# Talking-heads attention and two MoE layers on one core: the first two chunks relaid out by two queues, six score products moved behind the first mixing, one load of values moved to the front

## The chip, the core and the metric

The kernel runs on one core of a Trainium2 chip. Its engines are TensorE (PE: matmuls, with weight loads shown apart as PEld), VectorE (DVE), ScalarE (ACT), GpSimd (POOL) and SyncE (SP). SP, ACT and POOL can each start DMAs; in the profile an issue is listed under SPq, ACTq or POOL, and it is not counted as busy time of the engine. The metric is the device time of one execution in microseconds, the median of the timed runs.

## The reference

Everything is float32. For each of 2 batches, 12 heads, 448 positions and 64 numbers per head:

```python
scores = scale * q @ k.T                                 # per head
scores = einsum('bhij,hg->bgij', scores, w_pre)          # mix the 12 heads
attn   = softmax(scores)                                 # over j
attn   = einsum('bhij,hg->bgij', attn, w_post)           # mix them again
x      = attn @ v                                        # 896 tokens x 768
x = (silu(x @ w_gate) * (x @ w_val)) @ w_out             # 768 -> 1536 -> 768
h = x @ w_in ; x = (h * relu6(h + 3) / 6) @ w_out2       # 768 -> 2048 -> 768
```

The attention is less than the first third of the time; all that the change touches lies in its first steps.

## The kernel before

The program is written out engine by engine in the order in which the Python code issues it; no scheduler reorders it, and semaphores are put in where one engine reads what another writes. So the order of the code is the order on each engine.

**Attention, tile by tile.** Each batch is cut into four tiles of about 120 query rows, eight tiles in all (t = 0 to 7). `scores(t, c)` makes the products of q and k for head pair c (six pairs, c = 0 to 5) in two PSUM banks; `scores_out(t, c)` copies them to the SBUF tile `S` of that t, one head by DVE and one by ACT. There are two `S` tiles, used in turn, so tile 2 writes where tile 0 was. As heads have to be mixed, the heads of ten query rows (a chunk) must come to lie over the partitions of one matmul: `relayout(m)` copies eight rows' heads of chunk m from `S` to `sx` by one DMA (104 partitions, 182 KB, issued by SP), and `relayout_rest(m)` the last two rows' (24 partitions, 42 KB, issued by POOL). Below, the first is called the main relayout and the second the rest. Tile 0 has the chunks 0 to 9, tile 1 begins with chunk 10. Two chunks make a pair.

`next_engines(n)` is a tiny DMA by POOL that moves the place at which POOL's next DMA begins among the 16 DMA engines.

**The steps.** The loop at L615 runs over steps i from -2. In step i PE does `postmix(i)` (second mixing of pair i) and `premix(i + 2)` (first mixing of pair i + 2), DVE does `weights(i + 1)` and `row_max(i + 2)`, ACT does `exps(i + 1)`. For one pair the path is: both mains and both rests landed, `premix` on PE (four matmuls), `row_max` on DVE (two TENSOR_REDUCE, L252), `exps` on ACT (L261), `weights` on DVE (three small operations), `postmix` on PE (L287), `attn_out` (copies, L306), later `av` (L318). Other work hangs on named places in a step: `at_step(i, f, ..., place=...)`. The scores of tile 2 are made in steps 1 to 5, and its first copy to `S` must wait until all relayouts of tile 0 have landed.

**What is fixed before the loop.** The loads of q, k, the mixing weights and two of four pieces of v (`load_v(0, 0)` and `(0, 1)`, L139) are issued; then all scores of tiles 0 and 1 (L527 to L530); between them the relayouts of chunks 0 to 7 are issued. From step -2 on further relayouts follow, two or three per step; `scored[t]` (L555) is the step after which those of tile t may be issued, and the first one of a step waits for that step's `postmix`, the others for its `row_max`. The third and fourth piece of v are issued by ACT in steps 1 and 2, `load_q(3)` by ACT in step 3 (L594).

**Counters.** DMAs of SP and ACT use eight completion counters in turn (DMAHW0 to DMAHW7 in the listings). A DMA that gets a counter first waits until the DMA that had it before, eight earlier in the program, has landed. What stands behind such a DMA on its engine waits with it.

After the attention come the matmuls of the MoE layers (L441), to which nothing is done here.

Of the kernel before, what the change touches and what calls it, by code (L numbers as in the profile page):

```python
# [16 lines left out]
B, H, S, D = 2, 12, 448, 64  # L17
NT = B * S
DM = H * D
HP = H // 2  # L20
# [7 lines left out]
JC = 4  # L28
# [20 lines left out]
def kernel(  # L49
# [14 lines left out]
    nc = tc.nc  # L64
# [5 lines left out]
    def bank(name, tag):  # L70
        return ps.tile([128, 512], F32, name=name, tag=tag, bufs=BUFS[tag])
# [18 lines left out]
    small = kp.tile([128, 8], F32, name="small")  # L90
# [23 lines left out]
    def new_v(b):  # L114
        vs[b] = pv.tile([128, JC, H, D], F32, name=f"v{b}", tag="v")

    def load_v(b, j, eng=nc.scalar):
        eng.dma_start(
            out=vs[b][:, j].rearrange("p h d -> p (h d)"), in_=vv[b, :, j * DM : (j + 1) * DM]
        )  # L120
# [15 lines left out]
    nc.sync.dma_start(out=W2.rearrange("p g k -> p (g k)"), in_=w_post)  # L136
    load_q(2, eng=nc.sync)
    new_v(0)
    for j in range(2):  # L139
        load_v(0, j, nc.sync)  # L140

    Ss = [psc.tile([128, H + 1, S], F32, name=f"S{i}") for i in range(2)]
# [14 lines left out]
    stiles, pqk = {}, {}  # L157

    def scores(t, c, tags=("pqk", "pqk")):

        b, i = divmod(t, 4)
        n = ROWS[b][i]
        if c == 0:
            stiles[t] = Ss[t % 2]
        base = c * n
        p = [bank(f"pqk{t}_{c}_{e}", tags[e]) for e in range(2)]
        for s in range(2):
            lo, hi = 64 * s, min(64 * s + 64, n)
            for e in range(2):
                r = slice(64 * e, 64 * e + 64)  # L170
                nc.tensor.matmul(  # L171
                    p[e][lo:hi, :S],
                    lhsT=qs[t][r, base + lo : base + hi],
                    rhs=ks[b][r, c, :],
                    start=True,
                    stop=True,
                    tile_position=(64 * e, 64 * s),
                )
        for e in range(2):
            pqk[t, 2 * c + e] = p[e]  # L180

    def scores_out(t, c):
        n = ROWS[t // 4][t % 4]
        for e in range(2):
            h = 2 * c + e
            copy = nc.scalar.copy if e else nc.vector.tensor_copy
            copy(stiles[t][:n, h, :], pqk.pop((t, h))[:n, :S])  # L187

    sx = {}

    in_turn = mybir.DependencyInfo(mybir.DependencyClass.Sync, mybir.DependencyReason.DATA)

    def relayout(m, then=None):

        t, c = chunks[m]
        i, r = divmod(m, 2)  # L200
        if r == 0:
            sx[i] = psx.tile([128, 2, S], F32, name=f"sx{i}", tag="sx")
        rows = stiles[t][c : c + 7 * STRIDE + 1 : STRIDE, :, :]
        dma = nc.sync.dma_start(out=sx[i][0:104, r, :], in_=rows)
        if then:
            tc.add_manual_dep(dma.ins, then, in_turn, reason="a step's share of the DMA engines")

    def next_engines(n):

        to = 4 + n % 4  # L210
        nc.gpsimd.dma_start(
            out=small[0:24, to : to + 1], in_=small[0:8, 0:3].rearrange("p (h w) -> p h w", w=1)
        )

    next_engines(0)

    def relayout_rest(m):
        t, c = chunks[m]
        rows = stiles[t][c + 8 * STRIDE : c + 9 * STRIDE + 1 : STRIDE, :H, :]
        nc.gpsimd.dma_start(out=sx[m // 2][104:128, m % 2, :], in_=rows)  # L220
        if m % 4 == 3 and m + 1 < NCH:
            next_engines(m // 4 + 1)

# [105 lines left out]
    turns = cst.tile([1, 1], F32, name="turns")  # L329
# [189 lines left out]
    def keep_clock(n):  # L519

        p = ps.tile([128, 512], F32, name=f"clock{n}", tag="ppost", bufs=BUFS["ppost"])
        for _ in range(n):
            nc.tensor.matmul(p[:, :480], lhsT=ones[0], rhs=ones[1], start=True, stop=True)

    keep_clock(WARM)
    placed = 0
    for t in range(2):  # L527
        for c in range(HP):
            scores(t, c, (("pqk", "pqk"), ("ppre", "ppre"), ("ppost", "ppost"), ("ppre", "pav"))[(6 * t + c) % 4])
            scores_out(t, c)  # L530
        if t == 0:
            for _ in range(8):
                relayout(placed)
                relayout_rest(placed)
                placed += 1
    rests = placed

# [3 lines left out]
    def at_step(i, f, *args, place="end"):  # L541
        extra[i][place].append((f, args))
# [9 lines left out]
        else:  # L552
            at_step(now + 1, scores_out, t, c, place="S")

    scored = {0: -3, 1: -3}  # L555
    for t in range(2, 8):
        scored[t] = 6 * t - 7
        for c in range(HP):
            i = scored[t] - 5 + c
# [8 lines left out]
    for t, (begin, end) in enumerate(((5, 10), (11, 16), (17, 22), (23, 28), (29, 34), (35, 40), (41, 46))):  # L568
        busy = None
        for c in range(HP):  # L570
            i = begin + c * (end - begin + 1) // HP
            out = x_out if t < 6 else x_last
# [11 lines left out]
        if t < 6:  # L584
            step = 1 if t < 4 else 2
            i = split_at.setdefault(t, max(end + 1, split_at.get(t - 1, 0) + 4 // step))
# [4 lines left out]
    at_step(20, new_v, 1)  # L591
    for b in range(2):
        at_step(scored[4 * b + 3] + 1, new_x, b)
    loads = [(1, load_v, 0, 2), (2, load_v, 0, 3), (3, load_q, 3), (6, load_q, 4)]  # L594
    loads += [(7 + n, load_k, 1, n, n + 1) for n in range(HP)]
    loads += [(15, load_q, 5), (21, load_q, 6), (27, load_q, 7)]
    loads += [(20 + 2 * j, load_v, 1, j) for j in range(JC)]
# [17 lines left out]
    for i in range(-LOOK, NP):  # L615
# [36 lines left out]
        for m in ready[:1]:  # L652
            relayout(m, begun_at)
        run(i, "end")
        for m in ready[1:]:
            relayout(m, maxed)
        placed += len(ready)

        while rests < placed and rests // 2 <= i + LOOK + 4 and i > scored[chunks[rests][0]]:
            relayout_rest(rests)  # L660
            rests += 1
# [181 lines left out]
```

## Time and profile before

| | |
|---|---|
| time, median of 3 runs | 673.52 us (673.15 to 676.69) |
| the profiled execution | 671.94 us |
| its span, first to last instruction | 670.2 us |
| PE busy in the span | 659.1 us (98%) |
| granted TensorE clock, mean | 1.000 of full |

The span is what the rows below count in: microseconds from the first instruction. The 1.7 us between span and time of the execution lie around it. The profile names an instruction by its line, its engine and its operands; "idle before" and "<-" say how long the engine stood before it and which event ended that. The chain of work that ended last goes back from the last instruction, at each step to what released it.

### The profile page before, as it was taken

The page shows a single profiled execution, that of the slowest core. Times are in us where ns is not written, and L with a number is a line of the kernel's source. Part 1 is how long each engine was busy: PE and PEld are TensorE (multiplying, and loading weights), DVE is VectorE, ACT ScalarE, POOL GpSimd, SP SyncE. Part 2 cuts the span into 40 slices and gives each one's busy share as a digit, 9 for nine tenths or more (in the row PEclk, how much of TensorE's full clock was granted, in tenths as well). Part 3 has the DMA queues.
Part 4 walks back from the last instruction along what each step waited for, and adds up shares of the span by engine and source line. Part 5 has one row for each costly group of instructions (what it writes and reads, how often), then busy time and mean ns, then how long its engine had stood idle before and what let it go on. Part 6 is the DMA issues. An engine that isn't in the chain of part 4 may idle for free.

```text
span 670.2 us, 16126 instructions
## 1 busy us (share of the span) xinstructions
PE 659.1 (98%) x6680; PEld 561.8 (84%) x6680; DVE 499.8 (75%) x836; ACT 296.5 (44%) x603; POOL 160.4 (24%) x204
## 2 busy tenths in 40 slices
PE   8999999999999999999999999999999999999997
PEld 2456665666899999999999999999999998999996
DVE  4878888889278888887886666578888888775540
ACT  4567776777244343433432323244445543333220
POOL 3544466545111122111120000013333332000000
PEclk9999999999999999999999999999999999999999
DMA  7767576545024242332432434222223333554420
GB/s 253 218 200 210 178 219 192 181 142 198 3 94 141 95 141 95 112 124 95 135 100 95 132 104 134 102 94 97 94 95 101 119 96 100 178 155 122 145 67 27
DMA packets 35225, 86.87 MB, mean 130 GB/s; under 512 B 10096, under 2 KB 23040, under 8 KB 35152
## 3 DMA queue, kind: packets, MB, share of 16 engines
q1 hardware_dynamic: 21600, 71.43, 32.3%
q10 hardware_dynamic: 5616, 10.48, 5.1%
q0 software_dynamic: 7936, 3.94, 2.4%
q8 instruction: 52, 0.85, 0.6%
q14 instruction: 21, 0.17, 0.1%
HBM read 62.37 MB, written 2.75 MB: 97 GB/s over the span
## 4 chain that ended last, share of the span: by engine, by line
PE 94%; DMA 3%; DVE 2%; ACT 1%; issue 0%; ACTq 0%; SPq 0%; DVEq 0%
PE pi L441 17%; PE pp L441 17%; PE po L441 13%; PE pv L441 12%; PE pg L441 12%; PE pav L318 5%; PE ppost L287 5%; PE ppre L239 4%; PE pqk L171 4%; PE p L441 2%; PE pav L337 2%; DMA sx<-S 2%; DMA k<-in_k_dram 1%; ACT e L261 1%; DVE nm L252 0%
## 5 line engine op out<-in xcount | busy, mean ns | idle before, releaser
L441 PE MATMUL pp<-g,hp 128*128 128x448 f32 x384 | 107.9, 362 | 0.0
L703 POOL TENSOR_TENSOR g<-rl,g 128x448 fp32r<-128x448 f32 x32 | 41.4, 1313 | 167.9 <-ACT g L702 167.9
L441 PE MATMUL po<-u,ho 128*128 128x448 f32 x288 | 81.3, 363 | 0.0
L441 PEld LDWEIGHTS pp<-g,hp 128*128 128x128 f32 x384 | 71.9, 187 | 4.5 <-ACT hp L427 0.2
L261 ACT ACTIVATE e<-ppre,nm 128x448 f32<-128x448 f32 x90 | 56.3, 631 | 35.4 <-DVE nm L252 33.8
L441 PE MATMUL pp<-g,lp 128*128 128x448 f32 x192 | 69.7, 363 | 0.2 <-DVE lp L432 0.2
L441 PE MATMUL pi<-x2l,hi 128*128 128x448 f32 x192 | 69.7, 363 | 0.0
L441 PE MATMUL pi<-x2h,hi 128*128 128x448 f32 x192 | 69.6, 362 | 0.0
L441 PE MATMUL pi<-x2h,li 128*128 128x448 f32 x192 | 69.1, 360 | 0.0
L703 POOL TENSOR_TENSOR u<-sg,u 128x448 fp32r<-128x448 f32 x24 | 32.2, 1362 | 148.3 <-ACT u L702 148.3
L220 POOL DMA_DIRECT2D sx<-S x90 | 52.5, 584 | 49.5 <-issue 11.8
L441 PEld LDWEIGHTS po<-u,ho 128*128 128x128 f32 x288 | 54.1, 188 | 3.5
L252 DVE TENSOR_REDUCE nm<-ppre 128x1 f32<-128x448 f32 x90 | 51.9, 618 | 4.8 <-PE ppre L239 2.3
L287 PE MATMUL ppost<-wn,e 60*64 60x60 f32 x2520 | 51.0, 220 | 3.0 <-DVE wn L273 1.7
L441 PE MATMUL po<-u,lo 128*128 128x448 f32 x144 | 51.8, 360 | 0.0
L318 PEld LDWEIGHTS pav<-at,v 128*64 128x64 f32 x576 | 27.9, 136 | 28.4 <-ACT xs L360 14.2
L239 PE MATMUL ppre<-sx,W 64*64 64x448 f32 x360 | 49.7, 544 | 1.3 <-ACT S L187 0.6
L287 PEld LDWEIGHTS ppost<-wn,e 60*64 60x64 f32 x2520 | 45.1, 134 | 6.1 <-ACT at L306 2.0
L171 PE MATMUL pqk<-k,q 64*64 64x448 f32 (+3 forms) x384 | 47.8, 539 | 1.2 <-DMA k<-in_k_dram 0.6
L441 PE MATMUL pg<-xl,hg 128*128 128x448 f32 x132 | 47.9, 363 | 0.0
L441 PE MATMUL pv<-xl,hv 128*128 128x448 f32 x132 | 47.9, 363 | 0.0
L441 PE MATMUL pg<-xh,hg 128*128 128x448 f32 x132 | 47.8, 362 | 0.0
(98 smaller groups left out, 1399.1 us busy)
## 6 DMA issues: line engine op xcount, KB each, us to landing
sx<-S SPq DMA_DIRECT2D x90, 182.0 KB
ri<-in_moe_w_in_dram SPq DMA_DIRECT2D x16, 768.0 KB
ro<-in_moe_w_out_dram SPq DMA_DIRECT2D x12, 768.0 KB
rg<-in_moe_w_gate_dram SPq DMA_DIRECT2D x11, 768.0 KB
rv<-in_moe_w_val_dram SPq DMA_DIRECT2D x11, 768.0 KB
rp<-in_moe_w_out_dram SPq DMA_DIRECT2D x12, 640.0 KB
rp<-in_moe_w_out_dram SPq DMA_DIRECT2D x6, 768.0 KB
sx<-S POOLq DMA_DIRECT2D x90, 42.0 KB, 4.5
```

The costliest lines, as they stand in the source:

```text
L171: nc.tensor.matmul(p[e][lo:hi, :S], lhsT=qs[t][r, base + lo : base + hi], rhs=ks[b][r, c, :], start=True, stop=True, tile_position=(64 * e ...
L220: nc.gpsimd.dma_start(out=sx[m // 2][104:128, m % 2, :], in_=rows)
L239: nc.tensor.matmul(p[a][64 * r : 64 * r + 64, :S], lhsT=W1[rows, :], rhs=x[rows, r, :], start=True, stop=True, tile_position=(64 * a, 64 * r),
L252: top = nc.vector.tensor_reduce(nm[:, a : a + 1], pre[i][a][:, :S], AX.X, ALU.max, negate=True)
L261: nc.scalar.activation(e2[a], p[a][:, :S], AF.Exp, bias=nm[:, a : a + 1], scale=1.0, accum_out=sm[:, a : a + 1])
L287: mm = nc.tensor.matmul(p[s][64 * c : 64 * c + 64, at, :, :], lhsT=e2[a][rows, 64 * k : 64 * k + 64], rhs=wn[rows, a, :].rearrange("p (g k ...
L318: nc.tensor.matmul(p[64 * e : 64 * e + 64, : 2 * n], lhsT=vs[b][:, jc, h, :], rhs=ats[t][:, 2 * jc : 2 * jc + 2, h, :n], start=jc == 0, st ...
L337: mm = nc.tensor.matmul(pavs[t, c][64 * e : 64 * e + 64, a * n : a * n + n], lhsT=vs[b][rows, JC - 1, h, :], rhs=ats[t][rows, KB - 1, h, : ...
L441: nc.tensor.matmul(p[:, :S], lhsT=wt[:, kk, :], rhs=xx, start=start, stop=stop)
L703: eng.tensor_tensor(to[1], src, to[0].bitcast(F32), ALU.subtract)
```

## The change

Four edits, all in the first steps.

1. `load_v(0, 2)`, the third piece of v (384 KB), is issued by SP with the first two, ahead of the relayouts, and no longer by ACT in step 1.
2. The main relayout of chunk 1 is issued by ACT, behind its copies of tile 0; SP issues the main of chunk 0 and then, in POOL's place, the rest of chunk 0. The first `next_engines` moves 16 elements, no longer 24.
3. `scores(1, 5)`, the last of tile 1, is made by PE in step -2 behind `premix(0)`, and its copies by DVE and ACT in step -1. The PSUM banks of the scores are given by a table, since the banks come round in another order.
4. `scored[1]` goes from -3 to -1, so that the relayouts of tile 1 (chunk 10 on) are issued from step 0 on, no longer from step -1.

```diff
--- before.py
+++ after.py
@@ -136,7 +136,7 @@
     nc.sync.dma_start(out=W2.rearrange("p g k -> p (g k)"), in_=w_post)
     load_q(2, eng=nc.sync)
     new_v(0)
-    for j in range(2):
+    for j in range(JC - 1):
         load_v(0, j, nc.sync)
 
     Ss = [psc.tile([128, H + 1, S], F32, name=f"S{i}") for i in range(2)]
@@ -190,7 +190,7 @@
 
     in_turn = mybir.DependencyInfo(mybir.DependencyClass.Sync, mybir.DependencyReason.DATA)
 
-    def relayout(m, then=None):
+    def relayout(m, then=None, eng=nc.sync):
 
 
 
@@ -201,23 +201,23 @@
         if r == 0:
             sx[i] = psx.tile([128, 2, S], F32, name=f"sx{i}", tag="sx")
         rows = stiles[t][c : c + 7 * STRIDE + 1 : STRIDE, :, :]
-        dma = nc.sync.dma_start(out=sx[i][0:104, r, :], in_=rows)
+        dma = eng.dma_start(out=sx[i][0:104, r, :], in_=rows)
         if then:
             tc.add_manual_dep(dma.ins, then, in_turn, reason="a step's share of the DMA engines")
 
-    def next_engines(n):
+    def next_engines(n, turns=3):
 
         to = 4 + n % 4
         nc.gpsimd.dma_start(
-            out=small[0:24, to : to + 1], in_=small[0:8, 0:3].rearrange("p (h w) -> p h w", w=1)
+            out=small[0 : 8 * turns, to : to + 1], in_=small[0:8, 0:turns].rearrange("p (h w) -> p h w", w=1)
         )
 
-    next_engines(0)
-
-    def relayout_rest(m):
+    next_engines(0, 2)
+
+    def relayout_rest(m, eng=nc.gpsimd):
         t, c = chunks[m]
         rows = stiles[t][c + 8 * STRIDE : c + 9 * STRIDE + 1 : STRIDE, :H, :]
-        nc.gpsimd.dma_start(out=sx[m // 2][104:128, m % 2, :], in_=rows)
+        eng.dma_start(out=sx[m // 2][104:128, m % 2, :], in_=rows)
         if m % 4 == 3 and m + 1 < NCH:
             next_engines(m // 4 + 1)
 
@@ -524,14 +524,18 @@
 
     keep_clock(WARM)
     placed = 0
+    banks = [("pqk", "pqk"), ("ppre", "ppre"), ("ppost", "ppost"), ("ppre", "pav"), ("pqk", "pqk"), ("ppre", "ppre")]
+    banks += [("ppost", "ppost"), ("ppre", "pav"), ("pqk", "pqk"), ("ppost", "ppost"), ("pqk", "pqk"), ("ppost", "ppost")]
     for t in range(2):
         for c in range(HP):
-            scores(t, c, (("pqk", "pqk"), ("ppre", "ppre"), ("ppost", "ppost"), ("ppre", "pav"))[(6 * t + c) % 4])
+            if (t, c) == (1, HP - 1):
+                break
+            scores(t, c, banks[6 * t + c])
             scores_out(t, c)
         if t == 0:
             for _ in range(8):
-                relayout(placed)
-                relayout_rest(placed)
+                relayout(placed, eng=nc.scalar if placed == 1 else nc.sync)
+                relayout_rest(placed, eng=nc.sync if placed == 0 else nc.gpsimd)
                 placed += 1
     rests = placed
 
@@ -552,7 +556,9 @@
         else:
             at_step(now + 1, scores_out, t, c, place="S")
 
-    scored = {0: -3, 1: -3}
+    scored = {0: -3, 1: -1}
+    at_step(-2, scores, 1, HP - 1, banks[-1], place="av2")
+    at_step(-1, scores_out, 1, HP - 1, place="S")
     for t in range(2, 8):
         scored[t] = 6 * t - 7
         for c in range(HP):
@@ -591,7 +597,7 @@
     at_step(20, new_v, 1)
     for b in range(2):
         at_step(scored[4 * b + 3] + 1, new_x, b)
-    loads = [(1, load_v, 0, 2), (2, load_v, 0, 3), (3, load_q, 3), (6, load_q, 4)]
+    loads = [(2, load_v, 0, 3), (3, load_q, 3), (6, load_q, 4)]
     loads += [(7 + n, load_k, 1, n, n + 1) for n in range(HP)]
     loads += [(15, load_q, 5), (21, load_q, 6), (27, load_q, 7)]
     loads += [(20 + 2 * j, load_v, 1, j) for j in range(JC)]
```

On ACT, from the last copy of tile 0 to the first exponentials (`S_119`, `S_120` before are `S_120`, `S_121` now: tiles 0 and 1). Before:

```order
L187 COPY S_119<-pqk_5_1_180 118x448 [waits PE_49]
L187 COPY S_120<-pqk_0_1_210 120x448 [waits PE_49]
L187 COPY S_120<-pqk_1_1_218 120x448 [waits PE_49]
L187 COPY S_120<-pqk_2_1_226 120x448 [waits PE_49]
L187 COPY S_120<-pqk_3_1_234 120x448 [waits PE_49]
L187 COPY S_120<-pqk_4_1_242 120x448 [waits PE_49]
L187 COPY S_120<-pqk_5_1_250 120x448 [waits PE_49]
L261 ACTIVATE e_124,sm_271<-ppre_0_257,nm_263 128x448 [waits DVE_49]
L261 ACTIVATE e_125,sm_271<-ppre_1_258,nm_263 128x448 [waits DVE_49]
L261 ACTIVATE e_126,sm_294<-ppre_0_279,nm_285 128x448 [waits DVE_49]
```

And now:

```order
L187 COPY S_120<-pqk_5_1_181 118x448 [waits PE_49]
L204 DMA sx_188<-S_120 104x1x448 [waits DVE_49,DMAHW0_49,Activation_49,Pool_49]
L187 COPY S_121<-pqk_0_1_211 120x448 [waits PE_49]
L187 COPY S_121<-pqk_1_1_219 120x448 [waits PE_49]
L187 COPY S_121<-pqk_2_1_227 120x448 [waits PE_49]
L187 COPY S_121<-pqk_3_1_235 120x448 [waits PE_49]
L187 COPY S_121<-pqk_4_1_243 120x448 [waits PE_49]
L261 ACTIVATE e_125,sm_270<-ppre_0_250,nm_256 128x448 [waits DVE_49]
L261 ACTIVATE e_126,sm_270<-ppre_1_251,nm_256 128x448 [waits DVE_49]
L187 COPY S_121<-pqk_5_1_260 120x448 [waits PE_49]
```

A DMA issue now stands ahead of ACT's five remaining copies of tile 1, and the sixth copy stands behind the exponentials of pair 0.

On SP, from the loads of v to chunk 3 (each `sx` tile takes two chunks). Before:

```order
L118 DMA v_116<-in_v_dram 128x768 [waits DMAHW5_49]
L118 DMA v_116<-in_v_dram 128x768 [waits DMAHW6_49]
L204 DMA sx_187<-S_119 104x1x448 [waits DVE_49,DMAHW7_49,Activation_49,Pool_49]
L204 DMA sx_187<-S_119 104x1x448 [waits DMAHW0_49]
L204 DMA sx_192<-S_119 104x1x448 [waits DMAHW1_49]
L204 DMA sx_192<-S_119 104x1x448 [waits DMAHW2_49]
```

And now:

```order
L118 DMA v_116<-in_v_dram 128x768 [waits DMAHW5_49]
L118 DMA v_116<-in_v_dram 128x768 [waits DMAHW6_49]
L118 DMA v_116<-in_v_dram 128x768 [waits DMAHW7_49]
L204 DMA sx_188<-S_120 104x1x448 [waits DVE_49,DMAHW1_49,Activation_49,Pool_49]
L220 DMA sx_188<-S_120 24x1x448 [waits DMAHW2_49]
L204 DMA sx_193<-S_120 104x1x448 [waits DMAHW3_49]
L204 DMA sx_193<-S_120 104x1x448 [waits DMAHW4_49]
```

One more load stands ahead of chunk 0, and the small rest of chunk 0 has the place of chunk 1's main.

On SP, chunks 10 to 14 (the first five mains of tile 1), and, behind the dots, on ACT the load of q in step 3. Before:

```order
L204 DMA sx_288<-S_120 104x1x448 [waits DMAHW1_49,Activation_49,Pool_49]
L204 DMA sx_288<-S_120 104x1x448 [waits DMAHW2_49,DVE_49]
L204 DMA sx_344<-S_120 104x1x448 [waits DMASW2_49,DMAHW3_49,DMASW1_49,PE_49]
L204 DMA sx_344<-S_120 104x1x448 [waits DMAHW4_49,DVE_49]
L204 DMA sx_406<-S_120 104x1x448 [waits DMASW4_49,DMAHW5_49,DMASW3_49,PE_49]
...
L109 DMA q_535<-in_q_dram 128x714 [waits DMAHW5_49]
```

And now:

```order
L204 DMA sx_339<-S_121 104x1x448 [waits DVE_49,PE_49,DMAHW3_49,Activation_49,Pool_49]
L204 DMA sx_339<-S_121 104x1x448 [waits DMAHW4_49,DVE_49]
L204 DMA sx_342<-S_121 104x1x448 [waits DMAHW5_49,DMASW1_49]
L204 DMA sx_342<-S_121 104x1x448 [waits DMAHW6_49,PE_49]
L204 DMA sx_406<-S_121 104x1x448 [waits DMASW3_49,DMAHW7_49,DMASW2_49,DVE_49]
...
L109 DMA q_535<-in_q_dram 128x714 [waits DMAHW6_49]
```

Chunk 10 now waits for PE (`postmix(0)`), chunk 11 for `row_max(2)`; the load of q waits for the counter of chunk 13 (DMAHW6), where it waited for that of chunk 14 (DMAHW5).

## Rows read from the trace of the kernel before

**Rows 1.** The page: span, and the DMA engines' busy tenths in 40 slices.
```profile
span 670.2 us, 16126 instructions
...
DMA  7767576545024242332432434222223333554420
```

**Rows 2.** Busy us of each engine in two stretches, then clock, DMA share, GB/s.
```profile
0.00:40.00 40.00, 35.08 (x572) 15.00 (x572) 25.29 (x60) 22.13 (x53) 17.58 (x35) 1.00 0.74 234
40.00:660.00 620.00, 617.79 (x6086) 541.30 (x6079) 474.16 (x776) 273.45 (x548) 142.81 (x169) 1.00 0.39 124
```

**Rows 3.** The chain that ended last, 6 to 40 us: start, duration, what.
```profile
10.95 0.85 SPq L204
...
11.84 4.36 DMA sx<-S
...
16.25 0.98 PE ppre L239 x4
...
17.25 0.64 DVE nm L252
...
25.35 7.85 DMA sx<-S
...
33.23 0.33 ACTq L109
```

**Rows 4.** Timeline around the first relayouts: start, duration, engine, what, count.
```profile
7.60 0.81 SPq L118 DMA_DIRECT2D v<-in_v_dram  x2
...
10.96 0.54 ACT L187 COPY S<-pqk 120x448 f32<-120x448 f32 x1 [0.21 <-PE pqk L171]
...
11.84 1.67 SPq L204 DMA_DIRECT2D sx<-S  x2
```

**Rows 5.** Stretches of 1 or 2 us, columns as in rows 2.
```profile
9.00:11.00 2.00, 2.00 (x24) 0.70 (x20) 1.62 (x4) 1.35 (x4) 1.00 (x2) 1.00 0.99 328
...
12.00:14.00 2.00, 2.00 (x24) 0.70 (x20) 1.62 (x4) 1.35 (x4) 2.00 (x5) 1.00 0.47 153
...
18.00:20.00 2.00, 1.27 (x7) 0.30 (x6) 1.05 (x5) 1.25 (x4) 0.91 (x3) 1.00 0.65 219
...
26.00:28.00 2.00, 2.00 (x52) 0.95 (x43) 1.72 (x5) 2.00 (x6) 0.57 (x1) 1.00 0.86 233
```

**Rows 6.** Timeline 19 to 27 us: DVE, an issue by SP, ACT.
```profile
19.89 1.15 DVE L252 TENSOR_REDUCE nm<-ppre 128x1 f32<-128x448 f32 x2
...
21.99 1.07 SPq L204 DMA_DIRECT2D sx<-S  x1
...
22.52 1.15 DVE L252 TENSOR_REDUCE nm<-ppre 128x1 f32<-128x448 f32 x2
...
25.82 0.53 ACT L187 COPY S<-pqk 120x448 f32<-120x448 f32 x1 [0.77 <-DMA sx<-S]
25.83 0.34 ACTq L118 DMA_DIRECT2D v<-in_v_dram  x1
```

**Rows 7.** Timeline 29 to 37 us: the copies, the exponentials and PE.
```profile
29.45 1.22 PE L239 MATMUL ppre<-sx,W 64*64 64x448 f32 x6
...
31.28 1.15 DVE L252 TENSOR_REDUCE nm<-ppre 128x1 f32<-128x448 f32 x2
31.52 1.04 PE L287 MATMUL ppost<-wn,e 60*64 60x60 f32 x54
31.89 0.53 ACT L187 COPY S<-pqk 120x448 f32<-120x448 f32 x1 [0.77 <-PE pqk L171]
...
33.97 0.63 ACT L261 ACTIVATE e<-ppre,nm 128x448 f32<-128x448 f32 x1 [1.55 <-DVE at L306]
...
34.75 0.59 PE L239 MATMUL ppre<-sx,W 64*64 64x448 f32 x2 [0.56 <-ACT e L261]
...
36.20 0.97 PE L171 MATMUL pqk<-k,q 64*64 64x448 f32 x6 [0.48 <-ACT S L187]
```

**Rows 8.** Instructions of tile sx, 0 to 60 us: POOL's DMAs, issue to landing.
```profile
DMA to landing us min/median/max: 3.6/4.7/7.4
```

## Prediction before the run

> **What bounds the kernel now.** I read the page first, then a table of busy time by stretch, then the chain of waits, then the timeline of the first 40 us. The table settles how much can be moved. From 40 to 660 us PE is busy 617.8 of 620 us, and neither clock nor order changes there, so whatever the change wins or loses ahead of 40 us reaches the end as it is [rows 2]. In the first 40 us PE is busy 35.1 us, but a busy PE is not a full one there: in the chain the pieces are DMA, DVE and ACT as often as PE [rows 3]. The span is 670.2 us, the execution 671.94 us [rows 1].
>
> The chain shows two places at which something other than PE sets the pace. First, chunk 1's main relayout, second in SP's queue, is issued at 11.84 us and lands at 16.20; then `premix(0)` can go on (16.25), and `row_max(0)` starts at 17.25 [rows 3]. From there each pair waits for the one before it through DVE and ACT: `row_max(1)` starts at 19.89, `row_max(2)` at 22.52, 2.63 us apart [rows 6]. Second, a main issued at 25.35 lands only at 33.21, and then ACT issues a load at 33.23 [rows 3]. That load is `load_q(3)`: it waits for the completion counter of chunk 14, and all of ACT waits behind it. ACT ended its copy at 31.89 + 0.53 = 32.42 and the first half of `row_max(5)` was done at about 31.28 + 0.6 = 31.9, but the exponentials of pair 5 start at 33.97 [rows 7]. PE stands twice behind that: 0.56 us for ACT's exponentials (34.75) and 0.48 us for ACT's copy (36.20) [rows 7].
>
> **The change part by part.**
>
> *First relayouts and third piece of v, in one term, since they share the DMA engines.* What should be won: chunk 1's main starts beside chunk 0's, at 10.95 instead of 11.84, 0.89 us earlier [rows 3]. What speaks against: the mains seem bound by the rate of the transfers, not by their issue. SP's issue takes 1.67 us for two at 11.84 and 1.07 us for one at 21.99, back to back for most of the time between [rows 4, 6], and the DMA engines' mean share over 18 to 20 us is only 0.65 [rows 5], so either some engines are full and others not, or it is latency. Two transfers side by side on full engines end when the second would have ended anyway.
>
> The third piece of v goes ahead of chunk 0 in SP's queue. Two such pieces are issued in 0.81 us, so one more is 0.4 us at 8.4 us, when SP has nothing else to do before 10.95 [rows 3, 4]: nothing. Its transfer is 384 KB (393 KB in thousands); from 9 to 11 us the engines are full (0.99) and move 328 GB/s [rows 5], so 393 / 328 = 1.2 us more. Part of that falls into a lull: from 12 to 14 us the share is 0.47 [rows 5]. What does not is paid by chunk 0.
>
> The rest of chunk 0 by SP is not in the trace. Its issue costs between nothing and the 0.85 us of a main in its place [rows 3]; chunk 2 then goes out no later than before. Its landing, second in SP's queue, lies between a POOL rest's shortest 3.6 us after issue [rows 8] and a main's 4.36 [rows 3]: 15.4 to 16.2, not the last of the four.
>
> Term: from -0.9 (v hidden, chunk 1 wins all its earlier issue) to +1.2 (v delays all and nothing is won). I take +0.4, nearer to the upper half because the full engines of 9 to 11 us are the row right beside it.
>
> The Trainium skill has a rule on this, in "DMA: Bandwidth & Descriptors", section "Why a DMA increments its semaphore by 16 and not by 1": a copy runs on the largest number of engines up to 16 that divides the slowest dimension of both sides, and for SP and ACT those are always the lowest-numbered ones. With 8 rows to 104 partitions that makes 8, the same 8 for both queues; the share of 0.65 while SP never pauses fits half of the engines being full. By this rule side by side wins nothing and the term would lie between 0 and +1.2; without it, at -0.9 to 0 plus what v costs.
>
> *ACT's issue ahead of its copies.* At most 0.85 us on ACT before five copies of 0.54 us with 0.21 us idle between them [rows 3, 4]; 4 x 0.21 = 0.84 us of idle takes it up before the last one. PE's later scores wait a few tenths for banks, but then PE waits for the relayouts anyway: 0, at most +0.2.
>
> *The last scores behind `premix(0)`.* PE has them ready in a pause (PE is busy 1.27 of 2 us from 18 to 20 [rows 5]); they are 0.75 us of work by the distance between two copies (0.54 + 0.21 [rows 4]). DVE's copy falls between `row_max(0)`, which ends at 17.25 + 1.15 = 18.4 [rows 3, 6], and the start of `row_max(1)` at 19.89; ACT's between the exponentials of pair 0 and 1. The banks that `premix(0)` takes are free earlier. 0, from -0.1 to +0.3 if the copies push the weights.
>
> *Tile 1's relayouts a step later.* Chunk 11 waits for `row_max(2)`, which ends at 22.52 + 1.15 = 23.67, and so goes out at about 23.7 instead of 21.99 [rows 6]; with the 0.4 from above 24.1. Chunk 10 goes earlier, chunks 12 and 13 follow at about 25.1 and 26.1. SP has caught up by chunk 17. Chunk 11 is wanted by `premix(5)`, at 29.45 before [rows 7], 29.85 now: 5.7 us later; POOL's landings have a median of 4.7 and a worst of 7.4 us [rows 8], a main 4.36 and 7.85 [rows 3]. I take 0; if it took 7.4 it would cost 24.1 + 7.4 - 29.85 = 1.65.
>
> *The stall of ACT.* `load_q(3)` now waits for chunk 13, the first main of step 1 as chunk 14 was, issued at about 26.1. It may land by the time ACT comes to the load, 32.42 + 0.4 = 32.8, which leaves 6.7 us. Chunk 14 took 7.85 us [rows 3], but with a 384 KB load of v issued by ACT at 25.83 [rows 6] beside it (share 0.86 over 26 to 28 us [rows 5]). That load is now gone from there (1.2 us of full engines), and SP pauses up to 2 us before chunk 11, in which its queue drains. 7.85 - 1.2 = 6.65 without the pause, so I take the stall as gone: the exponentials of pair 5 start when ACT is free, 32.42 instead of 33.97 [rows 7], -1.55. The bounds are 0 (it lands as late) and -1.55. What is late next is ACT itself (exponentials, copy of the second mixing, copy to S, 36.20 - 33.97 = 2.2 us) and then PE: second mixing, scores, first mixing, some 2.6 us from 31.52, which still fit before.
>
> *Sum.* +0.4 + 0 + 0 + 0 - 1.55 = -1.15 us, on the execution of 671.94: 670.8. That execution lies 1.6 us under the median of the runs, so in terms of the median 673.52 - 1.15 = 672.4 us. The bounds add up to -0.9 - 0.1 - 1.55 = -2.55 and +1.2 + 0.2 + 0.3 + 1.65 = +3.35, which will hardly come together.
>
> **The rivals.**
>
> *A. Both parts work.* The first relayouts win: `premix(0)` comes 0.9 us earlier. For: the lull from 12 to 14 us has room. Against: `row_max(1)` needs chunk 3, which still goes out fourth by SP, and ACT's first copy of tile 2 waits for tile 0's last landing at 25.82 [rows 6] whatever came before, so at most 0.7 remains. -0.7 - 1.55 = -2.25, 671.3 us.
>
> *B. The stall stays, and all comes later: slower.* The relayouts of tile 1 are issued a step later, so chunk 13 at 26.1 stands where chunk 14 stood at 25.35. If a main there still takes 7.85 us, ACT's load waits until 33.95 + 0.02 instead of 33.23, and everything behind moves by +0.7: 674.2 us. It decides from 6.7 us on. For: that is the one main of this stretch whose landing the trace shows. Against: the load that was beside it is gone.
>
> *C. The stall goes but chunk 11 is late.* `premix(5)` begins at 31.5; 0.98 us later [rows 3] `row_max(5)` can start, and 0.6 us after that the exponentials of pair 5, at 33.1 instead of 33.97 [rows 7]: -0.9, 672.6 us.
>
> *D. The clock falls.* PE's pause ahead of `premix(0)` is 0.75 us longer than before, as the last scores no longer fill it, and 0.4 us more by the first term. In the sparse 18 to 20 us the granted clock stayed at 1.00, its level of 2.4 GHz [rows 5]. Should it go to 1.2 GHz until the steps fill up, four pieces of PE work of about 1 us on the path (0.98 for `premix`, 1.04 for `postmix` [rows 3, 7]) would take twice as long: +4 - 1.15, 676.4 us.
>
> *E. Nothing comes of it.* ACT's wait moves to another operand and v's delay eats the rest: 0, 673.5 us.
>
> **How the numbers follow.** Chances: forecast 0.45, A 0.2, B 0.14, C 0.1, D 0.04, E 0.07. Half a per cent is 3.4 us, which is about what a measurement of this kernel can tell from no change: under 670.1 us counts as faster, over 676.9 as slower. No case but D comes near. Faster needs all of A and a microsecond that I have not found: 0.06. Slower needs D or the upper bounds together: 0.05. Within: 0.89. For the range, cases A to C lie between 671.3 and 674.2; the upper bounds without the sum of all mishaps, and the spread of the runs (up to 3.2 us above the median, 0.4 below), widen it to 670.3 and 675.3.
>
> **What would show each step.** After: the first `row_max` between 17.3 and 18.0 us (A: 16.5; v's whole delay: 18.4). The DMA share from 12 to 14 us well above 0.47, from 26 to 28 below 0.86. ACT's load of q in step 3 issued during or right behind its copy and not more than 0.3 us after it, the exponentials of pair 5 at about 32.8 (B: 34.7). `premix(5)` without a wait for a DMA (C: with one of over 1 us). PE busy from about 36 us on as from 37 before, and from 40 us on the same total. The prediction is wrong if PE's total from 40 us on changes by over a microsecond, if `load_q(3)` still holds ACT, or if `row_max(0)` moves by more than a microsecond either way.

## The result, and the profile after

The changed kernel takes 678.22 us (median; 674.99 to 680.82), the kernel before 673.15 beside it: a ratio of 1.0069, 95% interval 1.0054 to 1.0084. By the ratio it is slower by 4.6 us (the medians lie 5.1 apart), where 672.4 was forecast and 675.3 was the upper end. The profiled execution of after is 678.22 us with a span of 676.4, against 671.94 and 670.2 [rows 1]; the granted clock is 1.00 in every stretch of both. Here and below a median is over all runs of a kernel, while a ratio leaves out two runs in a slower state (one of 1669.05 us, one of 738.64 us).

The page of after, for rows 1: span, and the DMA engines' busy tenths.

```profile
span 676.4 us, 16123 instructions
...
DMA  8666566445222323324233243313222333553420
```

Busy us of each engine by stretch (columns as in rows 2): four stretches of after, the first for the first of rows 2.

```profile
0.00:40.00 40.00, 35.25 (x572) 15.62 (x572) 25.67 (x61) 21.90 (x53) 16.92 (x34) 1.00 0.73 236
40.00:60.00 20.00, 20.00 (x556) 12.58 (x552) 16.69 (x49) 14.33 (x42) 8.56 (x15) 1.00 0.67 196
60.00:180.00 120.00, 111.87 (x3042) 74.26 (x3038) 95.57 (x282) 79.57 (x227) 60.46 (x98) 1.00 0.54 167
180.00:660.00 480.00, 479.81 (x2463) 448.45 (x2460) 361.39 (x445) 179.53 (x279) 73.54 (x56) 1.00 0.33 110
```

The last two of them in before:

```profile
60.00:180.00 120.00, 117.98 (x3130) 79.76 (x3125) 97.33 (x293) 80.60 (x233) 60.66 (x98) 1.00 0.54 167
180.00:660.00 480.00, 479.81 (x2404) 448.93 (x2403) 359.91 (x434) 178.54 (x273) 73.57 (x56) 1.00 0.34 110
```

PE's busy time in the first 40 us is nearly the same (35.25 and 35.08), and so is that after 180 us. From 60 to 180 us, where the steps of the attention run on and the diff edits nothing, PE idles 8.1 us in place of 2.0. That difference of 6.1 us is the whole of the 6.2 by which the spans differ. The DMA share there is 0.54 in both: as many bytes, no more work.

The chain of waits from 60 to 180 us says what PE idles for. First before, then after (share of the stretch by line, then the pieces of the chain that are DMAs):

```profile
by line: PE pav L318 23.3%; PE ppost L287 21.0%; PE ppre L239 19.0%; PE pqk L171 15.4%; PE pav L337 10.5%; PE p L441 4.4%; DVE nm L252 1.8%; issue 1.3%; DVE yv L490 1.2%; DVE at L306 1.1%; DVE wn L273 0.5%; DVE rc L270 0.3%; DVE rc L269 0.2
```

```profile
by line: PE pav L318 20.4%; PE ppost L287 18.7%; PE ppre L239 17.0%; PE pqk L171 13.5%; DMA sx<-S 10.4%; PE pav L337 9.0%; issue 3.5%; DVE nm L252 1.8%; DVE yv L490 1.2%; PE p L441 1.2%; DVE S L187 1.0%; DVE at L306 1.0%; DVE wn L273 0.5%; 
...
64.78 2.41 DMA sx<-S
98.96 10.08 DMA sx<-S
```

Before has no relayout in its chain there; after has two, of 2.41 and 10.08 us. The chain counts a DMA from its issue to its landing; what PE itself waited at the two places is 2.47 and 1.55 us. Both stand at a switch from tile to tile, where the first copies of a new tile's scores into a buffer `S` wait until the last relayouts out of that buffer have landed. The timeline of after, at the first of them and, behind the last dots, at the second:

```profile
64.78 0.59 POOL L220 DMA_DIRECT2D sx<-S  x1 [0.31 <-PE pav L337]
...
66.91 0.53 ACT L187 COPY S<-pqk 120x448 f32<-120x448 f32 x1 [1.86 <-DMA small<-small]
67.19 0.62 DVE L187 COPY S<-pqk 120x448 f32<-120x448 f32 x1 [3.05 <-DMA sx<-S]
...
67.75 0.06 DVE L348 MEMSET turns<- 1x1 f32 x1
67.89 0.27 PE L337 MATMUL pav<-at,v 64*64 64x60 f32 x2 [2.47 <-DVE turns L348]
...
109.38 0.53 ACT L187 COPY S<-pqk 119x448 f32<-119x448 f32 x1 [0.92 <-DMA sx<-S]
...
110.46 0.27 PE L337 MATMUL pav<-at,v 64*64 64x55 f32 x2 [1.55 <-DVE turns L348]
```

It is to be read from the end: PE waits 2.47 us for DVE's `turns` (67.75), which stands in DVE's order behind a copy that waited 3.05 us for a relayout. PE's row names DVE; the cause is the DMA for which that copy waited. All of PE's waits from 60 to 180 us (us in total, times, longest), before and then after:

```profile
PE ppost L287 <- issue: 1.3, 1, 1.3
PE pav L337 <- DVE turns L348: 0.7, 2, 0.5
```

```profile
PE pav L337 <- DVE turns L348: 4.5, 4, 2.5
PE ppost L287 <- issue: 3.6, 3, 2.4
```

So 3.8 of the 6.1 us stand behind `turns`. The other 2.3 are idle time that the profile puts down to nothing ("issue"); there is 4.7 us of it in the kernel with the shift by sixteen below, which is no slower than before, so it need not belong to the change.

The first 40 us, timeline of after, for rows 4, 6 and 7:

```profile
6.62 1.44 SPq L118 DMA_DIRECT2D v<-in_v_dram  x3
...
10.43 0.84 SPq L204 DMA_DIRECT2D sx<-S  x1
10.44 1.55 ACTq L204 DMA_DIRECT2D sx<-S  x1
11.32 0.65 SPq L220 DMA_DIRECT2D sx<-S  x1
...
15.76 0.62 DVE L252 TENSOR_REDUCE nm<-ppre 128x1 f32<-128x448 f32 x1 [0.61 <-PE ppre L239]
17.25 0.62 DVE L252 TENSOR_REDUCE nm<-ppre 128x1 f32<-128x448 f32 x1 [0.87 <-PE pqk L171]
19.45 1.16 DVE L252 TENSOR_REDUCE nm<-ppre 128x1 f32<-128x448 f32 x2
...
22.09 1.15 DVE L252 TENSOR_REDUCE nm<-ppre 128x1 f32<-128x448 f32 x2
...
25.61 0.53 ACT L187 COPY S<-pqk 120x448 f32<-120x448 f32 x1 [0.98 <-DMA sx<-S]
...
28.64 0.34 ACTq L118 DMA_DIRECT2D v<-in_v_dram  x1
...
31.68 0.33 ACTq L109 DMA_DIRECT2D q<-in_q_dram  x1
32.12 0.63 ACT L261 ACTIVATE e<-ppre,nm 128x448 f32<-128x448 f32 x1
...
35.25 0.73 PE L318 MATMUL pav<-at,v 128*64 128x100 f32 x12
37.45 0.26 PE L337 MATMUL pav<-at,v 64*64 64x50 f32 x2 [1.47 <-DMA v<-in_v_dram]
```

`row_max(1)` and `row_max(2)` come 0.44 and 0.43 us earlier than 19.89 and 22.52 [rows 6], and ACT no longer stalls at the load of q (exponentials of pair 5 at 32.12 for 33.97 [rows 7]). But the fourth piece of v, issued at 28.64, holds PE at 37.45.

### The profile page after: what moved, and what is told of

It reads as the page before. It is cut to its first block, busy times and chain, and to the rows that moved or that the text cites. A ratio compares the mean times of both kernels' runs of the same rounds, so it can differ in the third digit from the quotient of the medians.

```text
span 676.4 us, 16123 instructions
## 1 busy us (share of the span) xinstructions
PE 659.5 (97%) x6680; PEld 562.3 (83%) x6680; DVE 499.7 (74%) x836; ACT 296.2 (44%) x603; POOL 159.5 (24%) x203
## 4 chain that ended last, share of the span: by engine, by line
PE 75%; DVE 17%; DMA 4%; ACT 2%; issue 1%; SPq 0%; DVEq 0%; ACTq 0%
PE pp L441 15%; PE po L441 13%; PE pv L441 12%; PE pg L441 12%; DVE yi L490 9%; PE ppost L287 4%; PE pav L318 4%; PE ppre L239 4%; PE pqk L171 4%; DMA sx<-S 3%; DVE rl L733 2%; PE p L441 2%; PE pav L337 2%; DVE yp L490 2%; DVE li L432 2%; ACT hi L427 2%
## 5 line engine op out<-in xcount | busy, mean ns | idle before, releaser
L220 POOL DMA_DIRECT2D sx<-S x89 | 51.8, 582 | 53.8 <-issue 12.5
L171 PE MATMUL pqk<-k,q 64*64 64x448 f32 (+3 forms) x384 | 49.2, 547 | 0.8 <-ACT S L187 0.8
L441 PE MATMUL pv<-xh,hv 128*128 128x448 f32 x132 | 47.8, 362 | 0.0
```

Of the source, the lines that this page charges most:

```text
L171: nc.tensor.matmul(p[e][lo:hi, :S], lhsT=qs[t][r, base + lo : base + hi], rhs=ks[b][r, c, :], start=True, stop=True, tile_position=(64 * e ...
L220: eng.dma_start(out=sx[m // 2][104:128, m % 2, :], in_=rows)
L441: nc.tensor.matmul(p[:, :S], lhsT=wt[:, kk, :], rhs=xx, start=start, stop=stop)
```

## The experiments

The theory (H1): GpSimd's DMAs go to other DMA engines than before. They are the rests of the relayouts and the tiny DMAs of `next_engines`. The change sends one rest fewer through GpSimd and makes the first tiny DMA smaller, both in the first microseconds; if each DMA of that queue takes the engines that follow those of the last one, every later one is displaced, for the whole attention. The Trainium skill says so in "DMA: Bandwidth & Descriptors", section "Why a DMA increments its semaphore by 16 and not by 1": for k below 16 the queue of GpSimd takes k consecutive engines from a round-robin cursor, k being the largest number up to 16 that divides the slowest dimension of both sides, while SP and ACT always take the lowest-numbered k. The profile does not show which engine a packet ran on; what a displacement does to the time can be tried. Rivals: the other edits of the order (H2), the early piece of v or chunk 1's issue by ACT (H3).

**GpSimd's queue as before, the rest of the change kept.**

```diff
-    next_engines(0, 2)
+    next_engines(0)
-                relayout_rest(placed, eng=nc.sync if placed == 0 else nc.gpsimd)
+                relayout_rest(placed, eng=nc.gpsimd)
```

> The changed kernel with the two edits of GpSimd's queue undone: chunk 0's rest goes through GpSimd again, and the first tiny DMA moves 24 elements again. All the rest of the change stays. H1 (the loss of 6 to 8 us of TensorE idle time between 60 and 180 us comes from GpSimd's DMAs landing on other DMA engines than before, through one rest fewer and a smaller tiny DMA): the loss is gone, 671 to 674 us, ratio to before 0.997 to 1.001, and TensorE's busy time between 60 and 180 us is back within 1 us of before's. H2 (the moved scores, tile 1's later relayouts, the other lanes set it): still 676 to 680 us. H3 (the early third piece of values or chunk 1's issue on ScalarE sets it): still 676 to 680 us.

Measured: 672.99 us, ratio 0.9997 (0.9978 to 1.0015). The loss is gone with two lines; H2 and H3 fall.

**The kernel before with these two edits alone.**

```diff
-    next_engines(0)
+    next_engines(0, 2)
-                relayout_rest(placed)
+                relayout_rest(placed, eng=nc.sync if placed == 0 else nc.gpsimd)
```

> The kernel before with nothing but the two edits of GpSimd's queue: chunk 0's rest goes through SyncE behind its main relayout, and the first tiny DMA moves 16 elements. H1: nearly the whole loss comes with these two edits alone, 676 to 680 us, ratio 1.004 to 1.010, with stalls of TensorE at the switches from tile to tile after 60 us. H2 and H3: 672 to 674 us, no change beyond the half microsecond that the rest's place on SyncE can cost.

Measured: 680.19 us, 1.0111 (1.0084 to 1.0137). By the ratio they bring 7.5 us, all of the change's loss and more (the clock has a part in that, see behind the last run), with relayouts in the chain again (from 60 to 180 us):

```profile
96.77 8.11 DMA sx<-S
113.04 1.94 DMA sx<-S
```

**Ten elements in the first tiny DMA.**

```diff
-    next_engines(0, 2)
+    nc.gpsimd.dma_start(out=small[0:10, 4:5], in_=small[0:10, 0:1])
```

> The changed kernel whole, but its first tiny DMA moves 10 elements from 10 rows to 10 rows instead of 16 elements from 8 rows to 16. By the rule of the Trainium skill (DMA: Bandwidth & Descriptors, Why a DMA increments its semaphore by 16 and not by 1) a queue of GpSimd takes k consecutive engines from a round-robin cursor, k the largest number up to 16 that divides the slowest dimension of both sides. H1 with that rule: 10 engines for the tiny DMA and 2 for each of three rests are 16, as 8 and four times 2 were before, so every later DMA of GpSimd finds its engines of before again: 671 to 674 us. H1 with a cursor that goes on by elements: 10 and 3 times 8 are 34, 2 past a full turn, not the 8 of before: as slow as the changed kernel or between. H2 and H3: 676 to 680 us.

Measured: 681.4 us, 1.0132 (1.0109 to 1.0155): a miss. Either the cursor does not go by the k of the rows, or this copy has another k than 10. The Trainium skill, in the section named above, tells of direct copies by GpSimd's queue that take all 16 engines; no row here shows whether this is one. If it is, 16 and three rests of 2 end 6 past a full turn, an estimate by that rule under which a slow kernel is no surprise.

**One tiny DMA of 24 elements more, in the kernel before.**

```diff
+    next_engines(3)
     next_engines(0)
```

> The kernel before with one tiny DMA of 24 elements more on GpSimd's queue at the start, nothing else. H1, with the rule that k engines follow a cursor: 8 engines further, so every rest of the attention lands on the eight engines of the main relayouts instead of the other eight, and the kernel gets slower, 676 to 685 us. H1 with a cursor by elements: shifted by 24, that is 8 past a full turn, the same. H2 and H3: one more DMA of 96 bytes costs nothing that can be measured, 672 to 674 us.

Measured: 686.0 us, 1.0186 (1.0157 to 1.0215). A DMA of 96 bytes costs some 12.5 us (0.0186 of 673), 1.6 us of PE's busy time already in the first 40 us (33.44 for 35.08). In its chain from 60 to 180 us:

```profile
135.58 2.82 DMA sx<-S
159.55 5.16 DMA sx<-S
```

**Chunk 0's rest back on GpSimd, 16 elements kept.**

```diff
-                relayout_rest(placed, eng=nc.sync if placed == 0 else nc.gpsimd)
+                relayout_rest(placed, eng=nc.gpsimd)
```

> The changed kernel with chunk 0's rest back on GpSimd, but the first tiny DMA left at 16 elements from 8 rows. By k consecutive engines from a cursor (the Trainium skill, DMA: Bandwidth & Descriptors): 8 rows give 8 engines with 16 elements as with 24, so all of GpSimd's DMAs find their engines of before, 671 to 674 us. If the cursor goes on by elements, it is 8 short of before's, and the kernel is slow, 677 to 686 us. If neither, and the place of the rest on SyncE was the whole cause: 671 to 674 us too, and the next kernel tells.

Measured: 674.28 us, 1.001 (0.999 to 1.0031). The number of elements does not matter: both have 8 rows on one side. A cursor that goes on by elements falls here.

**An idle DMA in the rest's old place.**

```diff
-    next_engines(0, 2)
+    next_engines(0)
+    idle = cst.tile([128, S], F32, name="idle")
...
+        if m == 0:
+            nc.gpsimd.dma_start(out=idle[104:128, :], in_=rows)
```

> The changed kernel whole (chunk 0's rest on SyncE), with the first tiny DMA at 24 elements again and one DMA more on GpSimd's queue in the rest's old place: the same rows of the same shape, into rows of a buffer that nothing reads. Under any rule of the cursor GpSimd's DMAs are those of before, and only the rest's data goes by SyncE. Cursor theory: 670 to 674 us, TensorE's busy time between 60 and 180 us back at 117 us or more. If it is the rest's place on SyncE that costs: 676 to 681 us.

Measured: 673.34 us, 1.0007 (0.9985 to 1.0029). The rest goes by SP as in the change, and the loss is gone. So it is not the rest's place that costs but its absence from GpSimd's queue. PE from 60 to 180 us in this kernel (columns as above):

```profile
60.00:180.00 120.00, 119.00 (x3138) 80.16 (x3137) 97.23 (x294) 81.19 (x236) 60.53 (x98) 1.00 0.55 166
```

**Thirty elements from ten rows.**

```diff
-    next_engines(0, 2)
+    nc.gpsimd.dma_start(
+        out=small[0:30, 4:5], in_=small[0:10, 0:3].rearrange("p (h w) -> p h w", w=1)
+    )
```

> The changed kernel whole, its first tiny DMA with 30 elements from 10 rows of 3 (30 rows to 10, where the others have 24 to 8 or 16 to 8). By k engines from a cursor: 10 engines and three rests of 2 are 16, as the 8 and four rests of 2 were before, so every later DMA has its engines of before: 670 to 674 us. The earlier kernel with 10 elements from 10 rows to 10 was slow; the skill's page tells of direct copies that take all 16 engines, and equal rows on both sides may have been one. If the cursor goes on by elements: 30 and 24 are 54, 6 past a full turn and not 8: slow, 677 to 683 us.

Measured: 674.82 us, 1.0026 (1.0006 to 1.0046). By the rule of the Trainium skill, as an estimate, 10 engines and three rests of 2 make up the 16 of before. Most of the loss goes, without a DMA more. By the ratios 1.7 us are left, where the kernel with the idle DMA has 0.5 (1.0007); the two intervals overlap, and that rest stays open.

**The same, with the fourth piece of v a step earlier.**

```diff
-    loads = [(2, load_v, 0, 3), (3, load_q, 3), (6, load_q, 4)]
+    loads = [(1, load_v, 0, 3), (3, load_q, 3), (6, load_q, 4)]
```

> The same with 30 elements, and the fourth piece of values issued one step earlier, at step 1 in place of step 2: the 1.47 us that TensorE waits for that piece at 37.45 us of the changed kernel should go, if it lands some 2 us sooner. With the cursor theory: 669.5 to 673 us, 0.5 to 1.5 us under the kernel with 30 elements alone. Rival: the step's issue on ScalarE delays a copy there and costs as much as it brings, equal times.

Measured: 673.4 us, 1.0004 (0.9983 to 1.0025). Inconclusive: 1.4 us below the kernel with 30 elements alone, with overlapping intervals. PE no longer waits for that piece and is busy 36.60 us in the first 40 instead of 35.33, but only 17.96 of the 20 us that follow, instead of 20.00.

**24 elements, the rest still on SP.**

```diff
-    next_engines(0, 2)
+    next_engines(0)
```

> The changed kernel whole, chunk 0's rest on SyncE, with only the first tiny DMA back at 24 elements. It fills the fourth place of a table: rest on GpSimd with 24 elements (before) 673.0, with 16 elements 674.3, rest on SyncE with 16 elements 678.2. By k engines from a cursor 24 and 16 elements are the same (8 rows, 8 engines), and what shifts the cursor is the rest that is gone: as slow as the changed kernel, 676 to 680 us. If the cursor went on by elements, 24 and 24 would be shifted by 8 from before's: slower than the changed kernel, near the 686 us of the kernel with one tiny DMA more.

Measured: 678.04 us, 1.0062 (1.0037 to 1.0087), as slow as the change. The table is full: what decides is whether the rest goes through GpSimd, not 16 or 24. Nor is it the number of DMAs in GpSimd's queue, with whatever counters they take in turn: this kernel, the change and the kernel with 30 elements send the same number, and the last (1.0006 to 1.0046) lies below the change (1.0054 to 1.0084).

**A shift by four.**

```diff
+    nc.gpsimd.dma_start(
+        out=small[0:12, 7:8], in_=small[0:4, 0:3].rearrange("p (h w) -> p h w", w=1)
+    )
     next_engines(0)
```

> The kernel before with one tiny DMA more on GpSimd's queue at the start, of 12 elements from 4 rows: by k engines from a cursor a shift of 4, so two of four rests share the main relayouts' engines, where a shift of 8 had all four there (686.0) and the changed kernel, 2 short of a full turn, has one of four and a part of the tiny ones (678.2). Cursor theory with a price for each shared rest: between these, 677 to 684 us. Rival, that any tiny DMA more costs by its place in the queue and not by its engines: 686 as with the other one more.

Measured: 681.27 us, 1.0104 (1.0064 to 1.0144), between the change and the shift by eight; but the two edits alone, with the same order of the program as here and a shift of -2, have 1.0111, so a price for each shared rest is not shown. Relayouts are 18.5% of its chain from 60 to 180 us:

```profile
64.69 3.49 DMA sx<-S
102.68 9.40 DMA sx<-S
127.42 4.50 DMA sx<-S
153.48 4.77 DMA sx<-S
```

**A shift by sixteen.**

```diff
+    next_engines(2)
+    next_engines(3)
     next_engines(0)
```

> The kernel before with two tiny DMAs of 24 elements more on GpSimd's queue at the start. By k engines from a cursor that is 8 and 8, a full turn: 672 to 674 us, no change from before, though one such DMA alone made it 686.0. Rival, that tiny DMAs at the start cost by being there: 686 us or more.

Measured: 674.03 us, 0.9997 (0.9975 to 1.002). One tiny DMA more costs 12.5 us, two cost nothing: what matters is where they leave the cursor, and two of 8 close a turn of 16.

**A try for a version that beats both**: the idle DMA with 24 elements, and v's fourth piece at step 1 (the two diffs above together).

> A try for a version that beats both: the changed kernel with 24 elements, the idle DMA in the rest's old place on GpSimd (673.3 us so far), and the fourth piece of values at step 1. If the ramp's gain (the mixing of values at 36.3 us, where before has 37.10) reaches the end: 671 to 672.5 us. If the later waits at the switches from tile to tile take it back, as they seem to in the kernel with 30 elements: 673 to 674 us.

Measured: 673.66 us, 0.9997 (0.9974 to 1.0019). It beats the changed kernel, and ties with the one before.

Some medians lie up to 1 us past the end of what was expected (680.19, 686.0, 674.28, 674.82, 674.03); none reaches the range of the rival that it was to exclude.

Sorted by the shift of the cursor that the rule of the Trainium skill gives: 0 or 16, 673.0 to 674.8 us (seven kernels beside the one before); -2, 678.0 to 680.2 (the change and two more); 4, 681.3; 8, 686.0. The kernel with ten elements does not fit: with k = 10 its shift is 0, and it took 681.4. In no profile of the seven does the chain from 60 to 180 us hold a relayout; in each of the shifted ones, and in that with ten elements, it does. The stretch matters: the two of the seven with v's fourth piece at step 1 have a relayout in the chain shortly before it (4.98 us at 54.44, 5.05 us at 54.20).

PE's busy time in one stretch of one execution does not tell the kernels apart. Below are the shift by sixteen, which is as fast as before, and then 24 elements with the rest on SP, which is slow but loses its time from 40 to 60 us:

```profile
60.00:180.00 120.00, 114.90 (x3077) 76.97 (x3069) 95.11 (x285) 78.98 (x228) 60.46 (x98) 1.00 0.53 163
```

```profile
40.00:60.00 20.00, 17.34 (x480) 11.05 (x479) 15.08 (x42) 12.98 (x38) 9.12 (x16) 1.00 0.67 198
60.00:180.00 120.00, 117.08 (x3151) 78.53 (x3144) 97.52 (x294) 81.58 (x235) 60.53 (x98) 1.00 0.54 168
```

**The clock.** In four of the slow kernels TensorE's granted clock (last column but two) fell for some microseconds while PE waited or just after. In the kernel with one tiny DMA more:

```profile
104.00:108.00 4.00, 2.40 (x15) 1.11 (x16) 1.12 (x4) 0.06 (x1) 1.97 (x4) 0.68 0.54 193
108.00:112.00 4.00, 4.00 (x100) 2.10 (x92) 3.02 (x10) 2.44 (x7) 1.78 (x3) 0.89 0.70 209
112.00:116.00 4.00, 4.00 (x104) 2.51 (x102) 3.80 (x11) 2.83 (x8) 1.09 (x2) 1.00 0.29 55
```

A mean of 0.68 says that the clock was for a part of the stretch at the lower of its two levels, 1.2 in place of 2.4 GHz. PE's 6680 matmuls are busy 664.7 us in this execution and 659.1 in before. The mean granted clock is 0.996, and 0.4% of the span of 683.7 us is 2.7 us, an estimate. So of the 13.5 us by which the spans differ 5.6 are longer work and not waits, and the clock explains about half of these. The kernels with the two edits alone, with ten elements and with the shift by four show such a fall too (lowest stretch of 4 us: 0.68, 0.58, 0.77); the profile of the change does not. So the times of the slow kernels are no clean measure of the displacement: part of them is the clock.

## Why the prediction was wrong

The step that failed is the first: "From 40 to 660 us PE is busy 617.8 of 620 us, and neither clock nor order changes there, so whatever the change wins or loses ahead of 40 us reaches the end as it is". PE's total from 40 us on fell by 6.1 us, all between 60 and 180 us, where one microsecond had been named as a sign of being wrong. The diff edits no step there; what changed is the state that GpSimd's queue hands from one DMA to the next. I priced the rest's issue and landing on SP, and put what its absence does to the DMAs behind it in GpSimd's queue at nothing, without a reason; the experiments put that at the whole loss of 4.6 us. `next_engines`, whose name points at this state, I did not price at all; its own edit turned out to cost nothing (678.04 us with 24 elements, 678.22 with 16).

The rule of the Trainium skill that I weighed for the relayouts on SP and ACT has a second half, on the cursor of GpSimd's queue, which would have been the rival on the slow side. Worked out from that rule as an estimate, with a cursor that starts at the lowest engine: a main relayout (8 rows) takes 8 engines, always the same ones; a rest (2 rows) takes 2, a tiny DMA 8. In before 8 + 4 x 2 = 16 a round, so all rests find the eight engines that no main uses, and the tiny ones stand with the mains. In after the first round is 8 + 3 x 2 = 14, so one rest of four shares engines with the mains from then on; with a shift of 4, two; of 8, all four.

What the runs show is that the loss goes with the rest's place in GpSimd's queue, that two tiny DMAs of 8 rows make a full turn where one does not, and that 16 and 24 elements from the same rows act alike; the run with ten elements stays open. That shared engines make the landings late is not shown. The profile has no landing of single mains, and the rests' median landing from 60 to 180 us does not sort the kernels: 4.7, 3.8 and 4.9 us in after and with the shifts by four and eight, 4.3 in before and 4.8 with GpSimd's queue as before.

- *First relayouts and third piece of v* (+0.4, from -0.9 to +1.2): `row_max(1)` came 0.44 us earlier, but chunk 0 went out at 10.43 and not 10.95 [rows 3], so the whole execution ran 0.5 us ahead by then. From the issue on it is +0.1, within the bounds. `row_max(0)` moved more: its halves start at 15.76 and 17.25, while in before both run together from 17.25 (the row below). The 1.49 us of the first half are past the microsecond that the prediction named as a sign of being wrong, but they do not reach `row_max(1)`.

```profile
17.25 1.16 DVE L252 TENSOR_REDUCE nm<-ppre 128x1 f32<-128x448 f32 x2 [1.95 <-PE ppre L239]
```

- *ACT's issue ahead of its copies* (0 to +0.2): it took 1.55 us and not 0.85, and ACT's copies came that much later; PE waited 0.76 us for one (12.62), ahead of a wait for relayouts anyway.
- *Last scores moved; tile 1's relayouts a step later* (0 each): no wait of over a microsecond from either in the first 40 us. Chunk 11 is not late: PE's `premix` waits for relayouts add up to 0.6 us over the first 180 us of after.
- *The stall of ACT* (-1.55): the mechanism was right, the size was that of one execution. The stall is gone from the trace of after (32.12), and PE's mixing of values starts 1.85 us earlier (35.25 against 37.10 before). It is gone in all nine profiled executions of the new order, and it stands in all five of the old one: ACT idles ahead of the exponentials of pair 5 for 1.55 us in before, 0.84 with the shift by sixteen, 1.14, 2.32 and 2.36 in the three displaced ones. With the shift by sixteen chunk 14 takes 6.59 us and not 7.85, and the mixing starts at 35.71; the six kernels of the new order that are as fast as before start it between 35.37 and 36.85, so no gain shows there. What I did not name is what is late next in after: the fourth piece of v, 8.77 us from issue to landing, which takes 1.47 back. The old order with the shift by sixteen (a piece of the chain, then the timeline):

```profile
25.23 6.59 DMA sx<-S
```

```profile
31.84 0.33 ACTq L109 DMA_DIRECT2D q<-in_q_dram  x1
32.58 0.63 ACT L263 ACTIVATE e<-ppre,nm 128x448 f32<-128x448 f32 x1 [0.84 <-DVE S L187]
...
35.71 0.74 PE L320 MATMUL pav<-at,v 128*64 128x100 f32 x12
```

- *Sum* (-1.15): with GpSimd's queue as before, the change is worth 0.9997, that is -0.2 us (-1.5 to +1.0). The forecast's sign stays undecided; its size is inside the interval.
- *Rival D* (the clock falls) gives a time close to the measured one, but it is not it: the granted clock is 1.00 in every stretch of after. It did fall in four of the other slow kernels, as shown above.

## What to carry to other kernels

When a change takes a DMA off a queue or puts one on it, ask what the queue's later DMAs inherit: here a DMA of 96 bytes at the start decided over 12.5 us, spread over the attention. Price every edited line and every DMA that changes its queue; a name like `next_engines` says which state to look at, even where its own edit costs nothing. And the size of a stall in one execution is not its size in the next: ACT's was 0.84 to 2.36 us in five executions of the same order, so a term taken from one trace needs a range.

## What the runs showed of the hardware

GpSimd's DMAs carry a state from one to the next: one DMA of 24 elements more makes the kernel 1.9% slower, a second one restores it (0.9997). What counts is the rows that it is divided by, not its bytes: 16 and 24 elements from 8 rows act alike (674.28 and 672.99 with the rest on GpSimd, 678.22 and 678.04 without), while 30 from 10 rows make up for most of the missing rest (674.82). Ten elements from 10 rows to 10 do not (681.4), which stays open. The same relayouts, with the same DMA share of 0.54 from 60 to 180 us, stay out of the chain (GpSimd's queue as before, the rest of the change kept) or stand in it twice (the change), depending on that state alone.

TensorE's granted clock fell at such waits: 0.68 over 104 to 108 us in the kernel with one tiny DMA more, where PE was busy 2.40 of 4 us, 0.89 over the next 4 us and 1.00 from 112 us on. PE's matmuls were busy 5.6 us longer in that execution than in before.
